# The last block's seven products in another order, tanh in pieces, and unit building with earlier loads

## The chip, the cores and the metric

The kernel runs on one core of one Trainium2 chip. The metric is device time of one launch, in microseconds (us). Engines: TensorE (PE, with its weight loads as PEld), VectorE (DVE), ScalarE (ACT), GpSimd (POOL), and SyncE (SP), whose queue issues nearly all DMAs. Each engine works through its instructions in the order in which they stand.

## The reference

Three stages, all in float32:

```python
# attention with random features, 4 x 8 heads, 576 positions, 64 wide, 128 features
phi(x) = exp(x @ omega.T - |x|^2 / 2 - max) / sqrt(m)
num = phi(q) @ (phi(k).T @ v);  attn = num / (phi(q) @ sum(phi(k)) + 1e-6)
# experts: x is (2304, 512), 8 experts of width 1024
P = exp(x @ w_gate - max), normalized 8 times by rows and columns
out = sum_e P[:, e:e+1] * (relu(x @ w1[e]) @ w2[e])
# last block: 512 -> 2048 -> 512, weights come as float64
h = x @ w_in;  g = h - tanh(h);  return g @ w_out
```

## The kernel before

The 2304 tokens are three thirds of 768 (`stages`, with `s` the third). The attention runs first, then the experts for s = 0, 1, 2, then the last block for s = 0, 1, 2. A float32 product is made of three products of rounded halves: each operand is split into a high half (a cast on ScalarE) and a low half (a difference on GpSimd or VectorE); six matmuls of 384 columns are one `product` (L1255).

Each 2x2 block of products is done with seven products instead of eight (a scheme of the Strassen kind). The seven right operands (`x` units, 0 to 6) are made once per third by `xops`, the seven left ones (`u` units) once per weight block, and are kept in DRAM (`st1` for the experts, `st3` for the last block). Sums of the products give four tiles of 128 x 384, called 11, 12, 21 and 22.

*Unit building.* During the experts' last third (s = 2) the generator `build` (L1166) turns `w_in` from float64 into float32 and makes the `u` units of the last block, in 16 steps (f, c). A step loads two pieces (`rb`, L1176), converts each with `single` (L1115 to 1138: six VectorE instructions, one GpSimd, one ScalarE), makes four sums (L1195 to 1198), and makes seven units of 128 x 128 in tiles `ub`: cast on ScalarE (L1214), difference on GpSimd (L1206), store by `puts` (L1234). `rb` and `ub` share the tag `rs` of pool `rawp`, three slots. Each `yield` is a tick: `between` (L1816) calls `tick` twice after every product of the experts, 14 times for a quad of seven products, and `tick` moves the generators of loads (`weights`), of x units (`xops`; every eighth tick unless `pace[3]`) and of the background (`bg`) by one step. A building step has 19 ticks. So the order of the program is fixed when it is written out; nothing is scheduled on the chip. Meanwhile TensorE works through `quad7` and the experts' second layer (`group`, tile Y, L1436), whose running sums `seven` are copied into the bank first (L1428) and out of it after (L1452) on ScalarE.

*The last block.* For each s there are eight units n (`NF`), 24 in all. `tanh_quad` (L1579) runs seven products into three banks a, b, e. Between two of them `fill` may issue a second-layer group (`l2`, tile l, L1617: 12 matmuls of 512 columns, then an eviction on VectorE, L1644 or L1646). The groups of a pair of units run during the pair after it, three to a unit. Product 0 is copied from a to b on ScalarE (L1586), so that b starts from it. Then come the four tiles, each by `shrink` (L1544): h - tanh(h), with another formula for small |h|, for which a Relu (L1559) gives the mask of `copy_predicated` (L1562). `shrink` issues square, tanh, two more squares, Relu, and the VectorE or GpSimd steps in one go; cast and low half of a tile (`third`) are issued within the next tile's. For the tiles 22 and 21 ("spare"), which lie in SBUF, two steps (L1553, L1554) are on GpSimd, for 11 and 12, which lie in a bank, on VectorE. The `u` units are loaded by `weights` into 16 slots in the order in which they are used, the units of a pair ahead of its four second-layer tiles `v`.

## Time and profile before

| | us |
|---|---|
| median of 3 runs | 2386.59 (2385.42 to 2388.12) |
| the profiled execution | 2392.4, span 2390.6 |
| TensorE busy | 2091.4 (87% of the span) |
| VectorE busy | 1577.1 (66%) |
| GpSimd busy | 1521.3 (64%) |
| ScalarE busy | 1446.7 (61%) |
| mean granted TensorE clock | 0.938 of full speed |

The median of the runs is 5.8 us below the profiled execution. Shares of busy time are means over stages that have different limits; the windows below give them by stretch. The granted clock is in parts of full speed: 1.00 is the upper level, 2.4 GHz, and 0.50 would be the lower, 1.2 GHz, all the time. A line of a wait gives the engine that waits, the tile and line of its instruction, and what released it.

### The profile page before, as it was taken

To read this page: it belongs to the slowest core of one execution; us is meant where nothing else is said; L and a number is where in the kernel's file an instruction comes from. 1 tells how busy PE (TensorE), PEld (TensorE's weight loads), DVE (VectorE), ACT (ScalarE), POOL (GpSimd) and SP (SyncE) were. 2 spreads that over 40 slices of the span, in tenths; PEclk is the share of its full clock that TensorE was granted. 3 is DMA by queue.
4 is the path that set the end of the run, shared out by engine and by line. 5 is a ranking of instruction groups with operands and counts; after the bars stand their busy time and mean duration, and the time that the engine had idled before them with its cause. 6 is when DMAs were issued, how large, how long until landed. Compare 5 with 4: busy or idle time off the path is not lost. (4 is left out here: it accounts for less than half of the span.)

```text
span 2390.6 us, 37677 instructions
## 1 busy us (share of the span) xinstructions
PE 2091.4 (87%) x11264; PEld 1936.5 (81%) x11264; DVE 1577.1 (66%) x3013; ACT 1446.7 (61%) x3563; POOL 1521.3 (64%) x1959
## 2 busy tenths in 40 slices
PE   9989999999999999999987787778995677776868
PEld 7768888899989999999987777778985566676767
DVE  8885779898756576666766566565445666656555
ACT  7874333444347777777676566566775555555554
POOL 7867778778648888888765565556654444334332
PEclk9999999999999999999999888899997888888888
DMA  6548888888768899988986877776774543723341
GB/s 165 151 133 287 302 280 278 309 280 282 245 198 281 310 331 329 347 309 313 350 269 207 272 254 238 253 227 231 251 280 167 194 145 143 266 111 145 115 169 61
DMA packets 394219, 566.44 MB, mean 237 GB/s; under 512 B 75408, under 2 KB 184352, under 8 KB 394016
## 3 DMA queue, kind: packets, MB, share of 16 engines
q1 hardware_dynamic: 387872, 556.63, 68.1%
q10 hardware_dynamic: 6144, 7.40, 0.9%
q8 instruction: 91, 1.49, 0.3%
q14 instruction: 112, 0.92, 0.1%
HBM read 390.81 MB, written 173.09 MB: 236 GB/s over the span
## 5 line engine op out<-in xcount | busy, mean ns | idle before, releaser
L1436 PE MATMUL Y<-h,y 128*128 128x384 f32 x2394 | 512.6, 348 | 102.0 <-ACT Y L1428 101.4
L1261 PE MATMUL b<-x,u 128*128 128x384 f32 x2160 | 468.8, 354 | 143.2 <-ACT b L1586 134.6
L1261 PEld LDWEIGHTS b<-x,u 128*128 128x128 f32 x2160 | 406.6, 200 | 161.9 <-ACT b L1586 143.2
L1436 PEld LDWEIGHTS Y<-h,y 128*128 128x128 f32 x2394 | 440.1, 197 | 116.3 <-ACT Y L1428 115.5
L1617 PE MATMUL l<-v,h 128*128 128x512 f32 x2016 | 489.9, 395 | 2.6 <-ACT x L102 1.8
L1617 PEld LDWEIGHTS l<-v,h 128*128 128x128 f32 x2016 | 381.1, 190 | 80.4 <-ACT x L102 2.1
L1345 POOL TENSOR_TENSOR h<-t,h 128x384 fp32r<-128x384 f32 x223 | 232.2, 1041 | 194.3 <-ACT h L1342 158.4
L1452 ACT COPY seven<-Y 128x384 f32<-128x384 f32 x534 | 247.4, 481 | 148.2 <-PE Y L1436 143.9
L1261 PE MATMUL a<-x,u 128*128 128x384 f32 x1440 | 315.1, 357 | 22.9 <-DMA u<-st 16.7
L1261 PE MATMUL e<-x,u 128*128 128x384 f32 x1440 | 298.4, 343 | 6.7 <-DVE seven L1450 5.7
L1261 PEld LDWEIGHTS a<-x,u 128*128 128x128 f32 x1440 | 276.7, 204 | 28.4 <-DMA u<-st 19.5
L1261 PEld LDWEIGHTS e<-x,u 128*128 128x128 f32 x1440 | 262.6, 194 | 8.2 <-DVE seven L1450 6.2
L1428 ACT COPY Y<-seven 128x384 f32<-128x384 f32 x558 | 262.4, 487 | 4.2 <-DVE seven L1450 4.2
L1345 POOL TENSOR_TENSOR h<-h,h 128x384 fp32r<-128x384 f32 x192 | 201.8, 1054 | 62.4 <-ACT h L1342 51.8
L1568 POOL TENSOR_TENSOR h<-x,h 128x384 fp32r<-128x384 f32 x48 | 51.5, 1073 | 188.8 <-ACT h L1567 188.8
L105 POOL TENSOR_TENSOR v<-rs,v 128x256 fp32r<-128x256 f32 x160 | 123.0, 799 | 54.3 <-ACT v L102 43.1
L1553 POOL TENSOR_TENSOR th<-x,th 128x384 f32<-128x384 f32 x48 | 48.4, 1009 | 154.6 <-ACT th L1552 152.1
L1560 DVE SCALAR_TENSOR_TENSOR x<-t,x 128x384 f32<-128x384 f32 x48 | 56.5, 1178 | 117.5 <-POOL x L1554 117.5
L1342 ACT CAST h<-t 128x384 fp32r<-128x384 f32 x224 | 115.5, 517 | 29.2 <-DVE t L1338 15.6
L1654 DVE SCALAR_TENSOR_TENSOR acc<-l,pt,acc 128x512 f32<-128x512 f32 x144 | 104.7, 743 | 29.4 <-PE l L1617 27.6
L102 ACT CAST u<-s 128x256 fp32r<-128x256 f32 x128 | 49.4, 409 | 105.8 <-POOL u L105 42.0
L105 POOL TENSOR_TENSOR u<-s,u 128x256 fp32r<-128x256 f32 x128 | 97.4, 778 | 22.5 <-ACT u L102 20.1
(270 smaller groups left out, 3799.0 us busy)
## 6 DMA issues: line engine op xcount, KB each, us to landing
u<-st SPq DMA_DIRECT2D x616, 256.0 KB, 5.2
y<-st SPq DMA_DIRECT2D x336, 256.0 KB, 4.9
st<-u SPq DMA_DIRECT2D x224, 256.0 KB, 4.0
rs<-in_moe_w_dram SPq DMA_DIRECT2D x128, 256.0 KB, 4.9
st<-y SPq DMA_DIRECT2D x128, 256.0 KB, 5.8
st<-v SPq DMA_DIRECT2D x96, 256.0 KB, 5.2
rq<-in_moe_w_dram SPq DMA_DIRECT2D x32, 512.0 KB, 4.9
v<-st SPq DMA_DIRECT2D x32, 512.0 KB, 6.2
```

Source lines behind the costliest of these rows:

```text
L102: nc.scalar.copy(dst[:, 0], src)
L105: eng.tensor_tensor(dst[:, 1, i : i + w], src[:, i : i + w], dst[:, 0, i : i + w].bitcast(F32), ALU.subtract)
L1261: nc.tensor.matmul(ps[:, :TB], u[:, wi, c], x[:, xi, c], start=(start and m == 0), stop=(stop and m == 5), skip_group_check=True,)
L1342: nc.scalar.copy(H[k][:, 0], src)
L1345: eng.tensor_tensor(H[k][:, 1], src, H[k][:, 0].bitcast(F32), ALU.subtract)
L1428: nc.scalar.copy(cell[0], xacc[i][:, d])
L1436: nc.tensor.matmul(ps, uw[i, g][0][:, wi, d * P : (d + 1) * P], Hs[g][i][:, hi], start=(n == 0 and not cell), stop=(n == 3 * len(gs) - 1), ...
L1452: nc.scalar.copy(xacc[i][:, d], ps)
L1560: V.scalar_tensor_tensor(s, gb, B1, s, ALU.add, ALU.mult)
L1568: G.tensor_tensor(lo, s, hi.bitcast(F32), ALU.subtract)
L1617: nc.tensor.matmul(ps, hh[f][0][:, hi, t : t + P], u2[n + f][:, wi], start=(f == 0 and i == 0), stop=(f == len(hh) - 1 and i == 2),)
L1654: V.scalar_tensor_tensor(a, ps, p[:, e : e + 1], a, ALU.mult, ALU.add)
```

## The change

*Last block.* `ORDER` becomes 0, 2, 1, 4, 6, 3, 5. `first_product` issues product 0 and the copy to b; `following` issues it for the next unit between products 3 and 5 of this one. `shrink` becomes a class `Tile` whose steps (`even`, `odd`, `squares`, `mask`, `back`, `out`) are issued in pieces, tile 21 before 22, and the last steps of 22 and 12 in the next unit. Second-layer groups stand after products 2, 4 and the next unit's 0, one each. `useq` gives the loads of `u` units the new order.

*Building.* Three `rb` loads are started at the beginning, after the x units of this third are done, and load 2k + 3 + i follows the conversion of piece i of step k. Units are made three to a tile, in pool `xtp` (tag x, five slots, those of the x units' raw tiles) and stored by three DMAs instead of four; a step still has 19 ticks. The x units for the last block's first third are prepared when building is over (`xgo`), one step a tick (`pace[3]`); `convert` waits 16 ticks instead of 6.

```diff
-    ORDER = (0, 2, 1, 4, 3, 5, 6)
+    ORDER = (0, 2, 1, 4, 6, 3, 5)
+    NL = NF * NSB
+    useq = [
+        [(n, 0)] * (n < 2) + [(n, i) for i in range(1, 6)] + [(n + 1, 0)] * (0 < n < NL - 1) + [(n, 6)]
+        for n in range(NL)
+    ]
...
-                    jobs.append(("i", f, None, 0))
+                    jobs.append(("i", s * NF + f, None, 0))
...
-                while a not in built:
+                while len(built) < NF:
                     yield 1
-                for i in range(7):
+                for n, i in useq[a]:
                     while not free1(n1):
                         yield 1
-                    nc.sync.dma_start(tile1(n1).bitcast(F32), st3[a][:, i])
+                    nc.sync.dma_start(tile1(n1).bitcast(F32), st3[n % NF][:, i])
...
-        for _ in range(6 if fine else 1):
+        for _ in range(16 if fine else 1):
...
-        ld(0)
-        ld(1)
-        for _ in range(4):
+        for k in range(3):
+            ld(k)
+        while xbusy:
+            yield
+        for _ in range(10):
             yield
...
+                ld(2 * k + 3 + i)
...
-            for n in range(4):
-                u = rawp.tile([P, 2, 2, P], F32R, tag="rs", name=f"ub{k}_{n}", bufs=3)
-                xs = [src[i] for i in ORDER[2 * n : 2 * n + 2]]
+            for n in range(3):
+                xs = [src[i] for i in ORDER[3 * n : 3 * n + 3]]
+                u = xtp.tile([P, 3, 2, P], F32R, tag="x", name=f"ub{k}_{n}")
                 for o, x in enumerate(xs):
                     nc.scalar.copy(u[:, o, 0], x)
+                    if o == 1:
+                        yield
                 if put:
                     put()
                 put = finish(n - 1) if n else None
                 late.append((u, xs))
                 yield
-                if n == 2:
-                    put()
-                    put = None
-                    ld(2 * k + 2)
-            final = finish(3)
-            yield
+            final = finish(2)
             put()
             yield
             final()
-            ld(2 * k + 3)
...
+    class Tile:
+        def __init__(self, x, spare, name, key):
+            self.x, self.spare, self.name, self.key, self.h = x, spare, name, key, []
+            self.u, self.ga, self.gb = (tmp(i, f"t{i}_{name}") for i in range(3))
+            self.th = xtp.tile([P, TB], F32, tag="xo", name=f"th{name}", bufs=3)
+
+        def even(self):
+            nc.scalar.activation(self.u, self.x, AF.Square)
+            nc.scalar.activation(self.th, self.x, AF.Tanh)
+
+        def odd(self):
+            x, u, th = self.x, self.u, self.th
+            if self.spare:
+                self.s = x
+                nc.gpsimd.tensor_tensor(th, x, th, ALU.subtract)
+                nc.gpsimd.tensor_tensor(x, u, x, ALU.mult)
+            else:
+                self.s = tmp(3, f"t3_{self.name}")
+                nc.vector.tensor_tensor(self.s, u, x, ALU.mult)
+                nc.vector.tensor_tensor(th, x, th, ALU.subtract)
+
+        def squares(self):
+            nc.scalar.activation(self.gb, self.u, AF.Square, bias=bsq[:, 1:2])
+            nc.scalar.activation(self.ga, self.u, AF.Square, scale=CS, bias=bsq[:, 0:1])
+
+        def mask(self):
+            nc.scalar.activation(self.u, self.u, AF.Relu, bias=bsq[:, 2:3])
+
+        def back(self):
+            V, s = nc.vector, self.s
+            V.scalar_tensor_tensor(s, self.gb, B1, s, ALU.add, ALU.mult)
+            V.scalar_tensor_tensor(s, self.ga, A1, s, ALU.add, ALU.mult)
+            V.copy_predicated(s, self.u.bitcast(U32), self.th)
+
+        def out(self):
+            self.h.append(hslot(f"h{self.name}", self.key))
+            hi, lo = self.h[0][:, 0], self.h[0][:, 1]
+            nc.scalar.copy(hi, self.s)
+            nc.gpsimd.tensor_tensor(lo, self.s, hi.bitcast(F32), ALU.subtract)
+
+    lastq = []
+
+    def first_product(n, last):
+        a, b = qbank(f"a_{n}"), qbank(f"b_{n}")
+        product(a, 0, True, False, last)
+        nc.scalar.copy(b[:, :TB], a[:, :TB])
+        return a, b
+
+    def tanh_quad(n, key, last, ab, fill, following):
+        a, b = ab
+        e = qbank(f"e_{n}")
         A, B, EE = (x[:, :TB] for x in (a, b, e))
         V = nc.vector
+        if lxp:
+            x22, x21 = (lxp[0].tile([P, TB], F32, tag="x", name=f"x2{i}_{n}", bufs=3) for i in (2, 1))
+        else:
+            both = xtp.tile([P, 2, TB], F32, tag="x", name=f"x2_{n}")
+            x22, x21 = both[:, 0], both[:, 1]
+        b22, b12 = lastq or (None, None)
+        lastq.clear()
+        product(e, 2, True, False, last)
+        nc.scalar.copy(x22, EE)
+        if b22:
+            b22.out()
         fill(0)
+        product(b, 1, False, False, last)
+        nc.scalar.copy(x21, B)
+        if b12:
+            b12.mask()
+            b12.back()
         fill(1)
+        product(a, 4, False, True, last)
+        t11 = Tile(A, False, f"11_{n}", (*key, 0))
+        t11.even()
+        t11.odd()
+        t11.squares()
+        t11.mask()
+        t11.back()
+        if b12:
+            b12.out()
         fill(2)
+        product(e, 6, False, True, last)
+        t11.out()
+        V.tensor_tensor(x21, EE, x21, ALU.add)
+        t21 = Tile(x21, True, f"21_{n}", (*key, 0))
+        t21.even()
+        t21.odd()
+        t21.squares()
         fill(3)
         product(b, 3, False, False, last)
+        V.tensor_tensor(x22, B, x22, ALU.add)
+        t22 = Tile(x22, True, f"22_{n}", (*key, 1))
+        t22.even()
+        t22.odd()
+        t21.mask()
+        t22.squares()
+        t21.back()
         fill(4)
+        ab = following()
+        fill(5)
         product(b, 5, False, True, last)
+        t12 = Tile(B, False, f"12_{n}", (*key, 1))
+        t12.even()
+        t22.mask()
+        t22.back()
+        t21.out()
+        t12.odd()
+        t12.squares()
+        lastq.extend((t22, t12))
         fill(6)
+        return [[t11.h, t21.h], [t12.h, t22.h]], ab
 
...
-                pace[3] = Q < 2 or Q == NQ - 1
+                pace[3] = Q < 2 or Q == NQ - 1 or s == NSB - 1 and not bg
...
-                if Q == NQ // 4:
+                if Q == NQ // 4 and s < NSB - 1:
+                    xgo[0] += 1
+                if Q > 1 and s == NSB - 1 and not bg and xgo[0] < NSB:
                     xgo[0] += 1
...
+                    elif k in ((3, 5, 6) if turning else (0, 2, 5)):
...
+                def following():
+                    if not s and not n or s == NSB - 1 and n == NF - 1:
+                        return None
+                    over = n == NF - 1
+                    state["x0"] += 7 * over
+                    ab = first_product(f"{s}_{n + 1}", n == NF - 2)
+                    state["x0"] -= 7 * over
+                    return ab
+                if not s and n < 2:
+                    ab = first_product(f"{s}_{n}", False)
+                    if not n:
+                        second(1)
+                blocks, ab = tanh_quad(f"{s}_{n}", (s, n2), n == NF - 1, ab, fill, following)
```

On TensorE, around the turn from unit 5 to unit 6 of the last third, these rows stand before (a, b and e are the banks with their unit's number, l a second-layer group, u and x the units):

```order
L1261 MATMUL b_5_26699<-x_25733,u_26513 128x384 x6
L1261 MATMUL e_5_26698<-x_25799,u_26515 128x384 x6
L1261 MATMUL a_6_26907<-x_25053,u_26829 128x384 x6
L1261 MATMUL e_6_26908<-x_25585,u_26831 128x384 x6
L1261 MATMUL b_6_26909<-x_25609,u_26833 128x384 x6
L1261 MATMUL a_6_26907<-x_25643,u_26835 128x384 x6
L1617 MATMUL l_26959<-v_26541,h_2_4_26690 128x512 x3
```

And now:

```order
L1266 MATMUL e_5_26683<-x_25647,u_26518 128x384 x6
L1266 MATMUL b_5_26637<-x_25692,u_26520 128x384 x6
L1266 MATMUL a_6_26800<-x_25009,u_26522 128x384 x6
L1666 MATMUL l_26809<-v_26171,h_2_2_26376 128x512 x3
L1666 MATMUL l_26809<-v_26184,h_2_2_26326 128x512 x3
L1666 MATMUL l_26809<-v_26210,h_2_3_26576 128x512 x3
L1666 MATMUL l_26809<-v_26459,h_2_3_26509 128x512 x3
L1266 MATMUL b_5_26637<-x_25719,u_26524 128x384 x6
L1266 MATMUL e_6_26863<-x_25523,u_26849 128x384 x6
```

Product 0 of unit 6 (a_6) moved ahead of a second-layer group and the last product of unit 5.

On ScalarE, around the copy b<-a of unit 6, before (L1551 is the square, L1552 tanh, L1555 and L1556 the two squares with a bias, L1559 the Relu, L1567 the cast to the high half; t_21 and the like belong to the tile of that name):

```order
L1567 CAST h_2_5_26860<-x_2_5_26779 128x384
L1559 ACTIVATE t_12_2_5_26849<-t_12_2_5_26849,bsq 128x384
L1551 ACTIVATE t_21_2_5_26888<-x_2_5_26733 128x384
L1552 ACTIVATE th_2_5_26891<-x_2_5_26733 128x384
L1555 ACTIVATE t_21_2_5_26890<-t_21_2_5_26888,bsq 128x384
L1556 ACTIVATE t_21_2_5_26889<-t_21_2_5_26888,bsq 128x384
L1567 CAST h_2_5_26898<-t_12_2_5_26853 128x384
L1559 ACTIVATE t_21_2_5_26888<-t_21_2_5_26888,bsq 128x384
L1586 COPY b_6_26909<-a_6_26907 128x384
L1592 COPY x_2_6_26933<-b_6_26909 128x384
```

And now (L1556 square, L1557 tanh, L1571 and L1572 the two squares, L1575 the Relu, L1586 the cast, L1594 the copy):

```order
L1575 ACTIVATE t_21_2_5_26769<-t_21_2_5_26769,bsq 128x384
L1571 ACTIVATE t_22_2_5_26788<-t_22_2_5_26786,bsq 128x384
L1572 ACTIVATE t_22_2_5_26787<-t_22_2_5_26786,bsq 128x384
L1594 COPY b_6_26801<-a_6_26800 128x384
L1556 ACTIVATE t_12_2_5_26831<-b_5_26637 128x384
L1557 ACTIVATE th_2_5_26834<-b_5_26637 128x384
L1575 ACTIVATE t_22_2_5_26786<-t_22_2_5_26786,bsq 128x384
L1586 CAST h_2_5_26841<-x_2_5_26685 128x384
L1571 ACTIVATE t_12_2_5_26833<-t_12_2_5_26831,bsq 128x384
L1572 ACTIVATE t_12_2_5_26832<-t_12_2_5_26831,bsq 128x384
L1610 COPY x_2_6_26864<-e_6_26863 128x384
```

The copy of b_6 stood behind the Relu of tile 21, the last tile of unit 5; it now stands behind the Relu of tile 21 and two squares of tile 22, ahead of tile 12.

In the load queue, within one building step, before (rb is a load for building, st<-ub a store of units, y and u are loads for the experts):

```order
L1234 DMA st_1_144<-ub_0_17808 128x4x128
L1234 DMA st_1_144<-ub_1_17832 128x4x128
L1176 DMA rb_17864<-in_moe_w_in_dram 128x512
L299 DMA y_17900<-st_10_120 128x512
L277 DMA u_17902<-st_11_89 128x512
L299 DMA y_17900<-st_10_120 128x512
L277 DMA u_17905<-st_11_89 128x512
L1234 DMA st_1_144<-ub_2_17837 128x4x128
L1234 DMA st_1_144<-ub_3_17866 128x2x128
L1176 DMA rb_17909<-in_moe_w_in_dram 128x512
L299 DMA y_17956<-st_10_120 128x512
```

And now:

```order
L1181 DMA rb_18287<-in_moe_w_in_dram 128x512
L304 DMA y_18337<-st_12_122 128x512
L282 DMA u_18339<-st_13_91 128x512
L304 DMA y_18337<-st_11_121 128x512
L282 DMA u_18342<-st_13_91 128x512
L1238 DMA st_2_145<-ub_0_18314 128x6x128
L1238 DMA st_2_145<-ub_1_18344 128x6x128
L1238 DMA st_2_145<-ub_2_18377 128x2x128
L304 DMA y_18461<-st_12_122 128x512
L282 DMA u_18463<-st_14_92 128x512
```

Each rb stood right behind two stores of units; now the loads rb stand ahead of the stores, and the stores are three in a row.

## Rows read from the trace of the kernel before

**Rows 1.** Windows: start:end, length, busy us (count) by engine, clock, DMA, GB/s.

```profile
1230.00:1690.00 460.00, 361.02 (x1817) 348.05 (x1816) 276.94 (x502) 287.65 (x752) 273.57 (x339) 0.89 0.75 242
1700.00:1760.00 60.00, 60.00 (x348) 60.00 (x347) 24.75 (x45) 49.03 (x117) 36.53 (x37) 1.00 0.73 254
1836.00:2354.00 518.00, 379.67 (x1638) 336.58 (x1638) 308.70 (x455) 288.08 (x592) 206.48 (x207) 0.85 0.43 159
2185.00:2354.00 169.00, 128.26 (x546) 113.75 (x546) 95.45 (x146) 90.47 (x189) 58.12 (x58) 0.84 0.33 124
```

**Rows 2.** Waits, 1230 to 1690 us: engine, line, releaser; us, times, longest.

```profile
DVE cb L1122 <- DMA rb<-in_moe_w_in_dram: 103.6, 20, 13.1
...
PE Y L1436 <- ACT Y L1428: 94.6, 31, 9.6
...
ACT ub L1214 <- DMA st<-ub: 84.4, 16, 10.1
```

**Rows 3.** Line L1195: count, ns min/median/max, first and last start.

```profile
L1195 DVE TENSOR_TENSOR sb<-w x16: 275/420/1089, 1241.6 to 1680.6; 128x128 f32<-128x128 f32 x16
```

**Rows 4.** Waits, 1836 to 2354 us.

```profile
PE b L1261 <- ACT b L1586: 128.4, 21, 11.3
```

**Rows 5.** Chain of waits, 2269 to 2285 us: start, us, engine, tile, line.

```profile
2277.12 0.57 DVE t L1561
...
2277.78 0.59 DVE t L1562
...
2278.37 0.45 DVE x L1607
...
2279.86 1.01 POOL th L1553
...
2280.93 1.00 POOL x L1554
...
2282.57 0.39 ACT b L1586
```

**Rows 6.** Timeline of TensorE, 2264 to 2290 us; idle before, releaser.

```profile
2266.48 5.64 PE L1617 MATMUL l<-v,h 128*128 128x512 f32 x24
...
2271.96 1.23 PE L1261 MATMUL b<-x,u 128*128 128x384 f32 x6
...
2274.58 1.32 PE L1261 MATMUL a<-x,u 128*128 128x384 f32 x6 [0.34 <-DMA u<-st]
...
2283.00 2.29 PE L1261 MATMUL b<-x,u 128*128 128x384 f32 x6 [6.05 <-ACT b L1586]
```

**Rows 7.** Timeline of ScalarE: copies b<-a of three units.

```profile
1836.12 0.47 ACT L1586 COPY b<-a 128x384 f32<-128x384 f32 x1
...
2184.79 0.47 ACT L1586 COPY b<-a 128x384 f32<-128x384 f32 x1
...
2354.21 0.47 ACT L1586 COPY b<-a 128x384 f32<-128x384 f32 x1
```

**Rows 8.** DMA issues, 1230 to 1690 us: count, KB, us to landing.

```profile
st<-ub SPq DMA_DIRECT2D x48, 256.0 KB, 4.5
...
rb<-in_moe_w_in_dram SPq DMA_DIRECT2D x30, 256.0 KB, 3.2
...
xt<-xd SPq DMA_DIRECT2D x4, 384.0 KB, 8.0
```

**Rows 9.** Waits of the load queue, 1230 to 1690 us.

```profile
SPq L299 <- PE Y L1436: 98.8, 40, 7.6
```

**Rows 10.** Three lines on VectorE: ns min/median/max, first, last start.

```profile
L1560 DVE SCALAR_TENSOR_TENSOR x<-t,x x48: 548/1333/1361, 1793.5 to 2378.0; 128x384 f32<-128x384 f32 x48
...
L1125 DVE TENSOR_SCALAR cb<-cb x32: 293/296/1092, 1228.2 to 1675.7; 128x256 uint32<-128x256 uint32 x32
...
L1132 DVE SCALAR_TENSOR_TENSOR w<-rb,cb x32: 408/425/1211, 1231.7 to 1677.1; 128x256 f32<-128x256 uint32 x32
```

**Rows 11.** Groups, 1836 to 2354 us: count, busy, mean ns, idle before.

```profile
L1646 DVE TENSOR_TENSOR acc<-l,acc 128x512 f32<-128x512 f32 x44 | 30.0, 682 | 21.0 <-PE l L1617 21.0
```

More of the change, by code (lines that the diff above doesn't have):

```diff
@@ L1255, in product @@
     def product(ps, i, start, stop, last):
+        need(state["n1"], u1, "w")
         need(state["x0"] + i, ux, "x")
@@ L1542, in hslot @@
         return htile(name, kind == "k")
-    def shrink(x, spare, name, key):
-        h = []
-        V, G = nc.vector, nc.gpsimd
-        u, ga, gb = (tmp(i, f"t{i}_{name}") for i in range(3))
-        th = xtp.tile([P, TB], F32, tag="xo", name=f"th{name}", bufs=3)
-        s = x if spare else tmp(3, f"t3_{name}")
-        eng = G if spare else V
-        nc.scalar.activation(u, x, AF.Square)
-        nc.scalar.activation(th, x, AF.Tanh)
-        eng.tensor_tensor(th, x, th, ALU.subtract)
-        eng.tensor_tensor(s, u, x, ALU.mult)
-        nc.scalar.activation(gb, u, AF.Square, bias=bsq[:, 1:2])
-        nc.scalar.activation(ga, u, AF.Square, scale=CS, bias=bsq[:, 0:1])
-        if held:
-            held.pop()()
-        nc.scalar.activation(u, u, AF.Relu, bias=bsq[:, 2:3])
-        V.scalar_tensor_tensor(s, gb, B1, s, ALU.add, ALU.mult)
-        V.scalar_tensor_tensor(s, ga, A1, s, ALU.add, ALU.mult)
-        V.copy_predicated(s, u.bitcast(U32), th)
-        def third():
-            h.append(hslot(f"h{name}", key))
-            hi, lo = h[0][:, 0], h[0][:, 1]
-            nc.scalar.copy(hi, s)
-            G.tensor_tensor(lo, s, hi.bitcast(F32), ALU.subtract)
-        held.append(third)
-        return h
@@ L1585, in tanh_quad @@
-        product(a, 0, True, False, last)
-        nc.scalar.copy(B, A)
-        fill(0)
-        product(e, 2, True, False, last)
-        fill(1)
-        product(b, 1, False, False, last)
-        x21 = spare(0, "x21")
-        nc.scalar.copy(x21, B)
-        fill(2)
-        product(a, 4, False, True, last)
-        h11 = shrink(A, False, f"11_{n}", (*key, 0))
+        if lxp:
[3 more added lines that the diff above has]
+            x22, x21 = both[:, 0], both[:, 1]
@@ L1602, in tanh_quad @@
+        t22 = Tile(x22, True, f"22_{n}", (*key, 1))
[4 more added lines that the diff above has]
+        t21.back()
         fill(4)
+        ab = following()
+        fill(5)
         product(b, 5, False, True, last)
-        h12 = shrink(B, False, f"12_{n}", (*key, 1))
-        fill(5)
-        product(e, 6, False, True, last)
-        V.tensor_tensor(x21, EE, x21, ALU.add)
-        h21 = shrink(x21, True, f"21_{n}", (*key, 0))
+        t12 = Tile(B, False, f"12_{n}", (*key, 1))
@@ L1840, in performer_moe_kernel @@
                 turning = not s and n < 3
-                for i in range(7):
-                    need(state["n1"] + i, u1, "w")
                 def fill(k):
@@ L1846, in fill @@
                     if not s and not n:
-                        second((1, 2, 2, 1, 1, 1, 1)[k])
-                    elif not turning or k > 3:
-                        if k in (1, 3, 4):
-                            second(1)
-                        while k > 4 and len(ready) > (1 if odd else 4):
-                            second(1)
-                    if k == (3 if turning else 1):
-                        ready.extend(coming)
-                        coming.clear()
-                for j, h in enumerate(tanh_quad(f"{s}_{n}", (s, n2), n == NF - 1, fill)):
-                    hh[j].extend(h)
+                        second((2, 2, 1, 1, 1, 1, 1)[k])
+                    elif k in ((3, 5, 6) if turning else (0, 2, 5)):
[11 more added lines that the diff above has]
+                    if not n:
+                        second(1)
+                blocks, ab = tanh_quad(f"{s}_{n}", (s, n2), n == NF - 1, ab, fill, following)
+                for j in range(2):
+                    hh[j].extend(blocks[j])
                 if not s and not n:
@@ L1871, in performer_moe_kernel @@
             state["x0"] += 7
-    held.pop()()
-    second(len(ready))
-    for tt in (3, 4, 5, 0, 1, 2):
-        begun[st, tt] = lbank("l2") if tt > 2 else qbank("l2")
+    b22, b12 = lastq
+    b22.out()
+    b12.mask()
+    b12.back()
+    b12.out()
+    for tt in range(NTS):
+        begun[st, tt] = lbank("l2") if tt < 3 else qbank("l2")
         l2_mm(begun[st, tt], n2 - GF, hh[tt // 3], tt, range(2))
-    ready.extend(coming)
     second(len(ready))
```

23 lines of the change are left out of this document (5 added, 18 removed).

## The prediction

> **What bounds the kernel now.** I read the page's slices first, in which TensorE's digits and its granted clock fall in the second half, and then the windows by stretch, where the reader should look for matmuls per time [rows 1]. From 1700 to 1760 us the third block of the expert layer runs undisturbed: 348 matmuls in 60 us, 0.172 us each, granted clock 1.00. From 1230 to 1690 us the same loop runs with the unit building beside it: 1817 matmuls in 460 us, granted clock 0.89; at 0.172 us they would need 313 us. From 1836 to 2354 us, the last block, 1638 matmuls take 518 us at 0.85. These two stretches are what the change touches, and each has its own bound.
>
> In the building stretch, the waits say who ends the idle time [rows 2]: TensorE waits 94.6 us for ScalarE's copy of the sum into its bank (L1428). That copy is a short instruction behind others: ScalarE itself waits 84.4 us, 16 times, at the casts of the units (L1214) until a store of an earlier tile has landed, once in each building step. VectorE waits 103.6 us, 20 times, at the first conversion (L1122) for its load. One building step lasts (1680.6 - 1241.6) / 15 = 29.3 us [rows 3]; it holds 29.3 x 1817 / 460 = 116 matmuls, 19.9 us at full rate.
>
> In the last block TensorE waits 128.4 us in 21 units, 6.1 us each, for one ScalarE copy, b<-a (L1586) [rows 4]. The chain of waits tells why [rows 5]: the copy needs only product 0 of the new unit, but stands on ScalarE behind the Relu (L1559) of the previous unit's last tile, which waits for two GpSimd steps, which wait for tanh, which waits for the sum x21, which waits for VectorE. After such a wait the next product takes 2.29 us in place of 1.23 [rows 6]: half clock. A unit lasts (2354.21 - 2184.79) / 7 = 24.2 us in the last third and (2184.79 - 1836.12) / 14 = 24.9 us before [rows 7], against a full-rate need of 7 x 1.03 us for the products and 3 x 2.74 us for the second-layer groups (two of them lie between 2266.48 and 2271.96 [rows 6]): 15.4 us.
>
> **The change, part by part.** It adds and removes no arithmetic; per unit the counts of casts, squares, sums and products stay. So every gain is a wait that goes, and every cost a new one.
>
> *Building.* Three loads are started ahead, and load number k+3 is issued as soon as number k is converted. A load is then read two halves later, that is about one step of 19 ticks (1.03 us each at full rate) or 19.9 us after issue; it lands after 3.2 us [rows 8], and even behind the longest wait for a y unit's slot in the load queue, 7.6 us [rows 9], it is there. The unit tiles move from three slots that they shared with those loads to five slots; three tiles a step in five slots means reuse after 1.7 steps, some 33 us, against 4.5 us for a store to land [rows 8]. So both waits go entirely. What is late next is the pair GpSimd and VectorE. A VectorE step whose two inputs lie in SBUF takes 0.55 us alone and 1.33 where it meets GpSimd [rows 10]; the conversions L1125 and L1132 likewise take 0.29 and 0.41 us at the least, 1.09 and 1.21 at the most. So the one waits until the other's instruction ends, and their times add. Per step GpSimd is busy 273.6 / 460 x 29.3 = 17.4 us [rows 1]. VectorE's building steps cost at least 2 x (3 x 0.29 + 3 x 0.41) = 4.2 us, and four 128x128 sums at 0.29 (an estimate from L1125's size) 1.2 us, and the layer's own such step, 19/14 of it in a step at 0.55, 0.8: 6.2 us. Together 23.6 us, more than TensorE's 19.9. I take 25.0, the sum and 6% for turns that are not taken at once; 4.3 us x 16 steps = 68 us less. Bounds: 19.9 us if they overlapped (150 us less), and 29.3 if new waits ate it all (0).
>
> That both directions add is the point where a rule bears on the sum. The Trainium skill, page "SBUF — State Buffer", section "Who interferes with whom", says that the port pair of GpSimd and VectorE is an exclusive lock and that a VectorE instruction with two SBUF inputs contends with GpSimd, one with a single SBUF input (outside the two-port modes) does not. The rows above agree with the first half. By this rule the floor of a step is 23.6 us and the stretch can lose at most 5.7 x 16 = 91 us; without it 150.
>
> *The x units of the last block* are now prepared after the building, one step a tick. Their four loads land after 8.0 us [rows 8] and the first difference stands three ticks (3.1 us) behind the issue on VectorE's in-order queue: 5 us more, once, with everything behind it. Before, eight ticks lay between the steps.
>
> *The last block.* The copy b<-a now follows a product 0 that runs in the middle of the unit before, and stands behind two squares of tile 22. TensorE has b5, product 2, and a second-layer group, 4.8 us, to do before it needs the copy. So the 6.1 us go, and with them the half clock behind them. What is late next is VectorE's queue, which holds all four tiles in order. I follow it round one unit. The two sums: 1.1 us. Then it waits for x21, that is for square, tanh and two GpSimd steps: 2278.37 to 1.00 after 2280.93 is 3.6 us from the first sum's start [rows 5], 2.5 us beyond the sums; behind this wait stand the other tiles and the evictions, and for these TensorE's next groups. Then twelve dependent steps at 0.66 us from start to start (2277.12 to 2277.78 [rows 5]): 7.9. Four PSUM steps at 0.45 (as the sum at 2278.37): 1.8. Three evictions at 0.68 [rows 11]: 2.0. GpSimd has eight steps of 1.0 us in a unit; those that meet VectorE's chain are the two of tile 22 and two of the low halves: 4.0. Sum 19.3; I take 19.5 for the units of the last third. In the first two thirds the x units of the next third and the conversion of the second layer's weights run beside it, hidden in today's waits: GpSimd is busy (206.5 - 58.1) / 14 = 10.6 us a unit there against 58.1 / 7 = 8.3 in the last, VectorE 15.2 against 13.6 [rows 1], together 3.9 us more. Some of it fits into the 2.5 us of waiting; I put 1.5 us on top: 21.0. So 7 x 4.7 + 14 x 3.9 = 33 + 55 = 88 us less. Bounds: 15.4 us by TensorE, plus 0.7 because the first weights after a group now have one product less (1.03 us) of cover than at 2274.58, where they already came 0.34 us late [rows 6], per two units: 16.1; and 12.8 + 8 x 1.0 + 2.5 = 23.3 if all eight GpSimd steps stand in the way. The first two units and the end I leave as they are, with 15 us either way.
>
> Sum, against the profiled execution's 2392.4 us: -68 + 5 - 88 = -151, so 2241. The median is 2386.6, 5.8 us less than the profiled one; I forecast 2386.6 - 151 = 2236 us.
>
> **Rivals.**
> *The pair of GpSimd and VectorE binds harder.* A unit 22.5 us, a step 28 us: 21 x 2.2 + 16 x 1.3 = 67 us less, 2320. For it: today's tile steps L1560 in the SBUF form take 1.33 us at the median [rows 10], so nearly all of them meet GpSimd already. Against: there GpSimd has just been released by the same event, which the new order spreads.
> *TensorE becomes the bound.* A unit 17 us, a step 21 us: 21 x 7.7 + 16 x 8.3 = 294 less, 2093. For it: in stretches between two stalls the building stretch does run at full rate. Against: the sum of 23.6 us above.
> *The loads don't come earlier.* The load queue waits in order, 98.8 us for the slots of the y units (L299) [rows 9]; if new loads and stores stand behind such waits, building stays as it is and only the last block gains: 2386.6 + 5 - 88 = 2304. Against: 7.6 us is the longest of these, under the 19.9 us of lead.
> *Slower: the clock.* Today one long wait per unit costs half clock for one or two products [rows 6]. If the new order breaks this wait into several, and the granted clock of the last block stays near half, TensorE alone needs 2 x 15.4 = 31 us a unit: 23 x 6.4 = 147 more, less 68 and plus 5: 2471. It decides from a granted clock of 15.4 / 27.2 = 0.57 in the last block (there the loss equals the building's gain); today's is 0.85 [rows 1]. Against: products that follow waits of 0.34 us are not slow [rows 6]. The Trainium skill, "TensorE: Matmul & The Clock Gate", section "HAM oscillation — how this bites in real kernels", describes this: a loop whose every turn has a wait pays for the fall of the clock every turn. The trace of before agrees, with 2.29 us after 6.05 us of idling.
>
> **How the numbers follow.** Forecast 0.52, the pair 0.20, TensorE 0.13, loads 0.09, clock 0.06. From the pair I give 0.03 to no change at all. 0.2% (5 us) is about what a measurement of this kernel can tell from nothing. So faster 0.91, same 0.03, slower 0.06. The forecast alone spans 2190 to 2285. For 8 in 10 I leave out the far half of the TensorE case below and the clock above: 2130 to 2325.
>
> **What would show it.** Right: no long wait of the first conversion for rb and none of the unit casts for stores; the building steps 24 to 26 us apart; no long wait of TensorE for b<-a; units 18.5 to 21.5 us apart, VectorE or GpSimd busy for over 80% of them, the SBUF forms of the tile steps near 1 us. Wrong: units at 23 us or at 17, TensorE waiting for weights or x units where the last block begins for more than 20 us, or a granted clock there below 0.8.

## The result and the profile after

The changed kernel takes 2199.84 us (median of 4 runs, 2197.36 to 2202.42); the kernel before, on the same chip, 2387.36 us (2385.42 to 2389.31). The ratio is 0.9215, 95% interval 0.9199 to 0.9231: 187.5 us less. The forecast was 2236 us with a range of 2130 to 2325.

The changed kernel by stretch. The columns are those of [rows 1], the engines in the order PE, PEld, DVE, ACT, POOL; the first line is the building, the second the end of the experts behind it, the third 21 units of the last block.

```profile
1257.00:1593.00 336.00, 310.54 (x1709) 299.26 (x1709) 266.16 (x468) 266.95 (x707) 262.26 (x318) 0.98 0.86 289
1593.00:1685.00 92.00, 75.81 (x409) 73.23 (x408) 43.96 (x71) 63.80 (x153) 48.04 (x51) 0.94 0.83 292
...
1732.00:2159.00 427.00, 355.75 (x1640) 311.74 (x1641) 308.25 (x456) 284.17 (x596) 222.84 (x210) 0.91 0.52 192
```

The same 21 units took 518 us with 1638 matmuls in [rows 1]; now 427 with 1640, and the granted clock rose from 0.85 to 0.91. In the building it rose from 0.89 to 0.98.

The line of a building step's first sum (count, ns min/median/max, first and last start), which was L1195 in [rows 3]; and the waits from 1230 to 1620 us (engine, line, releaser: us, times, longest), which answer to [rows 2].

```profile
L1203 DVE TENSOR_TENSOR sb<-w x16: 276/464/1092, 1257.3 to 1592.8; 128x128 f32<-128x128 f32 x16
```

```profile
POOL h L1350 <- ACT h L1347: 78.1, 60, 5.6
...
PE Y L1441 <- ACT Y L1433: 23.2, 20, 3.3
...
DVE cb L1127 <- DMA rb<-in_moe_w_in_dram: 3.5, 1, 3.5
```

A step now lasts (1592.8 - 1257.3) / 15 = 22.4 us in place of 29.3. The wait of ScalarE's casts for stores (84.4 us) is gone, that of VectorE for its loads is down from 103.6 us to one of 3.5, and TensorE's for ScalarE's copy from 94.6 to 23.2.

Three of the 24 copies b<-a in the timeline of ScalarE (start, us, engine, line), the first, the third and the last, and behind them the first of before; [rows 7] has the third and the last of before.

```profile
1684.76 0.46 ACT L1594 COPY b<-a 128x384 f32<-128x384 f32 x1 [1.27 <-PE a L1266]
...
1732.86 0.47 ACT L1594 COPY b<-a 128x384 f32<-128x384 f32 x1
...
2158.38 0.47 ACT L1594 COPY b<-a 128x384 f32<-128x384 f32 x1
```

```profile
1773.09 0.46 ACT L1586 COPY b<-a 128x384 f32<-128x384 f32 x1 [0.95 <-PE a L1261]
```

A unit lasts (2158.38 - 1732.86) / 21 = 20.3 us on the average, before (2354.21 - 1836.12) / 21 = 24.7. The waits from 1732 to 2159 us:

```profile
DVE x L1579 <- POOL x L1564: 59.1, 22, 3.3
...
PE e L1266 <- DMA u<-st: 48.5, 10, 10.4
...
PE b L1266 <- DVE x L1639: 8.0, 4, 3.7
...
PE l L1666 <- ACT h L1586: 6.3, 4, 1.8
...
PE b L1266 <- ACT b L1594: 2.5, 1, 2.5
```

The wait of [rows 4], 128.4 us in 21 units, is down to one of 2.5 us. TensorE's largest is a new one: product 2 at the start of a pair of units waits for its unit u, ten times. The chain of waits ahead of the longest of these (start, us, what) shows whom the load had waited for:

```profile
1899.47 1.17 DVE x L1580
...
1901.21 0.69 DVE acc L1695
...
1901.92 0.33 SPq L1708
...
1902.35 0.38 SPq L334
...
1902.78 4.43 DMA u<-st
...
1907.26 2.29 PE e L1266 x6
```

L1708 is a store of finished rows, which waits for VectorE's sum; L334 is the fourth v load of a pair, which waits for its ring slot; the u loads of the next pair stand behind both in SP's queue. In this chain the store's wait ended last; L1708 stands there only at the ends of thirds. The queue's own waits from 1732 to 2159 us (line, releaser: us, times, longest) name what holds it elsewhere:

```profile
SPq L334 <- PE l L1666: 78.5, 5, 26.6
...
SPq L155 <- ACT v L107: 42.5, 6, 21.7
```

The v load waits for a second-layer group to free its slot. In the first third the v tiles are still made on the core; there L155, the load of a v tile's source, stands in its place. And product 2, once its weights are there, takes 2.29 us in place of 1.23: the granted clock from 1907.3 to 1909.5 us is 0.50, the lower level.

### The profile page after: what moved, and what is told of

Read it like the earlier page. It is cut to its first block, busy times and chain, and to the rows that moved or that the text cites. A ratio compares the mean times of both kernels' runs of the same rounds, so it can differ in the third digit from the quotient of the medians.

```text
span 2197.3 us, 37735 instructions
## 1 busy us (share of the span) xinstructions
PE 2035.7 (93%) x11264; PEld 1880.2 (86%) x11264; DVE 1588.4 (72%) x3013; ACT 1437.0 (65%) x3563; POOL 1537.9 (70%) x1959
## 4 chain that ended last, share of the span: by engine, by line
PE 58%; DVE 12%; POOL 12%; DMA 7%; issue 5%; ACT 4%; SPq 1%; DVEq 0%; POOLq 0%; ACTq 0%
PE l L1666 15%; PE Y L1441 13%; PE b L1266 11%; PE e L1266 8%; PE a L1266 7%; DMA u<-st 2%; PE X L1441 2%; POOL h L1350 2%; POOL tmp L596 2%; POOL eq L756 1%; DVE x L1579 1%; DMA y<-st 1%; DVE x L1580 1%; DMA xd<-seven 1%; POOL h L1587 1%
## 5 line engine op out<-in xcount | busy, mean ns | idle before, releaser
L1441 PE MATMUL Y<-h,y 128*128 128x384 f32 x2394 | 497.0, 340 | 43.7 <-ACT Y L1433 38.2
L1666 PE MATMUL l<-v,h 128*128 128x512 f32 x2016 | 500.2, 399 | 14.6 <-ACT h L1586 6.3
L1441 PEld LDWEIGHTS Y<-h,y 128*128 128x128 f32 x2394 | 423.6, 190 | 59.0 <-ACT Y L1433 50.2
L1266 PE MATMUL b<-x,u 128*128 128x384 f32 x2160 | 442.5, 340 | 19.6 <-DVE x L1639 9.0
L1266 PEld LDWEIGHTS b<-x,u 128*128 128x128 f32 x2160 | 385.8, 190 | 32.4 <-DVE x L1639 11.8
L1266 PE MATMUL e<-x,u 128*128 128x384 f32 x1440 | 299.9, 344 | 58.4 <-DMA u<-st 48.5
L1350 POOL TENSOR_TENSOR h<-t,h 128x384 fp32r<-128x384 f32 x223 | 232.7, 1044 | 145.1 <-ACT h L1347 120.4
L1266 PE MATMUL a<-x,u 128*128 128x384 f32 x1440 | 293.0, 338 | 3.2 <-DMA u<-st 1.7
L1266 PEld LDWEIGHTS a<-x,u 128*128 128x128 f32 x1440 | 256.3, 190 | 5.5 <-POOL u L110 1.6
L1587 POOL TENSOR_TENSOR h<-t,h 128x384 fp32r<-128x384 f32 x48 | 51.6, 1074 | 112.0 <-ACT h L1586 106.9
L1587 POOL TENSOR_TENSOR h<-x,h 128x384 fp32r<-128x384 f32 x48 | 55.2, 1149 | 97.0 <-ACT h L1586 94.6
L110 POOL TENSOR_TENSOR u<-s,u 128x256 fp32r<-128x256 f32 x128 | 98.2, 783 | 22.6 <-ACT u L107 22.3
L1347 ACT CAST h<-h 128x384 fp32r<-128x384 f32 x192 | 99.0, 516 | 7.5 <-POOL h L1398 5.8
```

Of the source, the lines that this page charges most:

```text
L110: eng.tensor_tensor(dst[:, 1, i : i + w], src[:, i : i + w], dst[:, 0, i : i + w].bitcast(F32), ALU.subtract)
L1266: nc.tensor.matmul(ps[:, :TB], u[:, wi, c], x[:, xi, c], start=(start and m == 0), stop=(stop and m == 5), skip_group_check=True,)
L1347: nc.scalar.copy(H[k][:, 0], src)
L1350: eng.tensor_tensor(H[k][:, 1], src, H[k][:, 0].bitcast(F32), ALU.subtract)
L1441: nc.tensor.matmul(ps, uw[i, g][0][:, wi, d * P : (d + 1) * P], Hs[g][i][:, hi], start=(n == 0 and not cell), stop=(n == 3 * len(gs) - 1), ...
L1587: nc.gpsimd.tensor_tensor(lo, self.s, hi.bitcast(F32), ALU.subtract)
```

## The experiments

**Each part alone.** The first kernel has the new building and the old last block (old order of products, tiles and groups); the second has the new last block and the old building. The lines below are from their edits against the kernel before: the change of `ORDER` is in the second alone, and the line of `useq`, which keeps the old order of the loads, is the first's.

```diff
-    ORDER = (0, 2, 1, 4, 6, 3, 5)
+    ORDER = (0, 2, 1, 4, 3, 5, 6)
...
+    useq = [[(n, i) for i in range(7)] for n in range(NL)]
```

> The new building of the units with the old last block. Theory A (the two edits stand in different stretches and add up): the first b<-a copy of the last block comes 88 us earlier than before (1773 to about 1685), the part behind it keeps its 617 us, the time is about 2387 - 88 = 2299 us, steps of building 22.4 us apart as in the kernel with both edits, granted clock of the building stretch .97 against .89. Rival B (part of the gain of the building is really the last block's, since its loads and x units share the same queue): the part behind the first copy takes under 600 us too, and the time is under 2280.

> The new order of the seven products and of the tanh steps with the old building of the units. Theory A (additive): the building keeps 29.3 us per step, the last block's part behind the first b<-a copy falls from 617 to about 512 us, the time is about 2387 - 105 = 2282 us. Rival B (the new order needs the units that the new building has ready earlier, or the x units that it prepares after building): the last block gains under 80 us, the time is over 2307.

New building alone: 2306.5 us, ratio 0.9665 (0.9651 to 0.968). New last block alone: 2283.0 us, ratio 0.9574 (0.9558 to 0.959). The two losses, 0.0335 and 0.0426, add up to 0.9239 against 0.9215 measured with both, whose interval reaches to 0.9231; theory A holds but for a few us. These kernels were timed on several chips, each beside the kernel before, so small differences are given by the ratios too. First, third and last copy b<-a with the new building alone, and then with the new last block alone:

```profile
1683.14 0.46 ACT L1587 COPY b<-a 128x384 f32<-128x384 f32 x1 [0.55 <-PE a L1262]
...
1745.37 0.47 ACT L1587 COPY b<-a 128x384 f32<-128x384 f32 x1
...
2263.48 0.47 ACT L1587 COPY b<-a 128x384 f32<-128x384 f32 x1
```

```profile
1766.08 0.46 ACT L1595 COPY b<-a 128x384 f32<-128x384 f32 x1 [1.03 <-PE a L1267]
...
1814.43 0.47 ACT L1595 COPY b<-a 128x384 f32<-128x384 f32 x1
...
2242.45 0.47 ACT L1595 COPY b<-a 128x384 f32<-128x384 f32 x1
```

Before, the first copy came at 1773.09 and the third 63.0 us later. With the new building the first comes 90 us earlier, the units keep their 24.7 us; with the new order the first two units take 48.4 us in place of 63.0 and the others 20.4.

**The wait for u.** The next kernel has both parts and lists the loads of a pair's first unit ahead of the fourth v load of the pair before; the one after it also holds the output stores back.

```diff
                 for f in range(g * GF, (g + 1) * GF):
+                    if f == (g + 1) * GF - 1 and p + 1 < NSB * NGM:
+                        jobs.append(("i", 2 * p + 2, None, 0))
...
-            nc.sync.dma_start(out[r : r + P, :], a)
+            stores.append([6, out[r : r + P, :], a])
```

> Both edits, and the loads of a pair's first unit stand in SP's queue before the fourth second-layer (v) load instead of behind it. Theory A (the ten waits of TensorE for u units, 48.5 us, come from SP's queue, where the v load waits for its slot): these waits fall under 10 us in all, the median unit stays 17.5 to 18 us, the time is 2200 - 35 to 45 = 2155 to 2165 us. Rival B (VectorE's queue is the floor at 19.5 us a unit, as the prediction had it): the waits turn into waits of b for x on VectorE, the mean of the 21 units stays above 19.5 and the time is above 2185. Rival C (the transfers themselves are late, or the v loads now come late): waits of l for v of over 20 us appear, time 2180 or more.

> As the kernel before it in this list, and the twelve output stores of the first two thirds are held back by six ticks (about a unit) in SP's queue, so that they don't stand there waiting for VectorE's sums. Theory A (the waits of 9 to 10 us at the thirds' boundaries, 1907 and 2068, are longer than the others since the queue also waits for the stores' sums): another 0 to 10 us, 2150 to 2160. Rival B (with the loads ahead of the blocked v load nothing waits behind the stores): within 3 us of the kernel before it.

2192.1 us, ratio 0.9188 (0.9174 to 0.9202), and 2187.1, ratio 0.9168 (0.9155 to 0.9182). That is 8 and 13 us below the changed kernel (6 and 11 by the ratios; the first interval just meets that of the changed kernel), where theory A expected 35 to 45 for the first; the second step's 5 us lie within the intervals. The waits of TensorE for u were taken away, but others came in their place, those of the second-layer groups. From 1650 to 2180 us of the first of the two:

```profile
PE l L1670 <- ACT h L1590: 27.8, 8, 4.6
...
PE b L1270 <- DVE x L1643: 11.8, 7, 4.2
...
PE l L1670 <- DMA v<-st: 11.4, 2, 6.0
```

None of the three theories names the first of these: at the place where the u load was late, the first group of a pair would have waited for its tile h anyway. h is the tile that the unit before finishes last (L1590 is the cast to its high half). So the next two kernels move the groups one place back, first in the even units, then in all.

```diff
-                    elif k in ((3, 5, 6) if turning else (0, 2, 5)):
+                    elif k in ((3, 5, 6) if turning else (0, 2, 5) if odd else (1, 3, 5)):
...
+                    elif k in ((3, 5, 6) if turning else (1, 3, 5)):
```

> The kernel with the loads ahead and the output stores held back (2187 us), and in the even units of the last block the three second-layer groups stand after the products 1, 4... of the order (places 1, 3, 5) instead of places 0, 2, 5. Theory A (with the loads there in time, the first group of a pair waits for the tile h that the unit before finishes last, 31 us in ten waits of l for ACT's copy of h): these waits fall under 10 us and the time to 2160 to 2172 us. Rival B (VectorE's queue is what is late, and the wait only moves to b or e): the sum of TensorE's waits on VectorE and ACT stays, time 2180 to 2190. Rival C (the later group frees the v slot later and the wait for v comes back): waits of l for v over 15 us.

> The same with places 1, 3, 5 in the odd units too. Theory A: the odd units' groups had no wait, so nothing more is gained, within 5 us of the kernel with the even units alone. Rival B: the groups beside VectorE's longest stretch help there as well, 5 to 15 us faster. Rival C: two products side by side at the start of each odd unit make b wait for the reading of its bank, 5 to 15 us slower.

2161.9 us, ratio 0.906 (0.9047 to 0.9072), and 2156.3, ratio 0.9041 (0.9028 to 0.9053). Theory A held for the first. The second is 6 us faster, between A and B of its expectation, but the intervals overlap. Two windows of the last block of the faster one:

```profile
1850.00:2030.00 180.00, 165.27 (x777) 143.16 (x778) 149.01 (x217) 129.78 (x277) 100.10 (x92) 0.97 0.59 217
2030.00:2120.00 90.00, 85.00 (x412) 73.53 (x411) 74.17 (x112) 66.64 (x144) 46.03 (x43) 1.00 0.46 167
```

TensorE is busy for 92 and 94% of them at a granted clock of 0.97 and 1.00. Its third copy b<-a starts at 1727.74 us and its last at 2115.93: 18.5 us a unit. The waits for b<-a come back in part there: 20.2 us in 16, the longest 2.9, from 1720 to 2120 us. This is the fastest version but for one that measured the same, told of below.

**What sets the building step.** One kernel computes each of the seven low halves twice on GpSimd; one leaves the tiles in their new pool and puts the loads back to their old places; one computes the four sums on VectorE three times.

```diff
                 for o, x in enumerate(xs):
                     G.tensor_tensor(u[:, o, 1], x, u[:, o, 0].bitcast(F32), ALU.subtract)
+                    G.tensor_tensor(u[:, o, 1], x, u[:, o, 0].bitcast(F32), ALU.subtract)
...
-                ld(2 * k + 3 + i)
...
+            ld(2 * k + 2)
             final = finish(2)
...
+            for _ in range(3):
+                V.tensor_tensor(s1, a21, a22, ALU.add)
```

> The changed kernel with each of the seven low halves of a building step computed twice on GpSimd (same result), 7 x 0.50 = 3.5 us more of GpSimd's time per step. Theory A (TensorE sets the step of 22.4 us, busy 310 of 336 us there; GpSimd and VectorE have room): steps of 22.4 to 23.0 us, time 2200 to 2210. Rival B (the times of GpSimd and VectorE add up at their port and set the step, as the prediction had it): steps of 25 to 26 us, time 2240 to 2260.

> The changed kernel with the ub tiles in their new pool, but the loads of the source tiles at their old places (two ahead, issued at the end of a step). Theory A (both waits of before came from the three slots that loads and ub tiles shared; with the loads alone in them the old places are early enough): no wait of VectorE for a load over 3 us, steps of 22.4 to 23 us, time 2200 to 2210. Rival B (a load takes longer to land than the old place leaves it, so the loads ahead are what helps): waits of cb for rb of 3 to 5 us come back in most steps, steps of 25 to 27 us, time 2235 to 2270.

> The changed kernel with the four sums of a building step on VectorE (both inputs in SBUF, 0.28 us each at the least) computed three times over, 2.24 us more of VectorE's time per step. Theory A (GpSimd's time and that of VectorE's steps with SBUF inputs alone add up and set the step of 22.4 us; the kernel with twice the low halves on GpSimd grew by 3.45 us a step for 3.2 to 3.5 added): steps of 24.4 to 25.2 us, time 2230 to 2245. Rival B (GpSimd's own queue sets the step and VectorE has room beside it): steps under 23 us, time under 2212. Rival C (each added step costs the mean that the records show, 0.4 to 0.6 us, so the chain of handing over is what grows): steps of 26 to 27.5 us, time over 2255.

2260.1 us (ratio 0.947, 0.9457 to 0.9483), 2257.1 (0.9457, 0.9444 to 0.947) and 2245.2 (0.9416, 0.9396 to 0.9437). The first sum's line in each of the three, which gives steps of 25.85, 26.06 and 25.1 us (in the third it counts all 48 sums, and its last start is of a third repeat, 1.9 us after the first):

```profile
L1203 DVE TENSOR_TENSOR sb<-w x16: 279/457/1097, 1255.8 to 1643.5; 128x128 f32<-128x128 f32 x16
```

```profile
L1202 DVE TENSOR_TENSOR sb<-w x16: 276/464/1103, 1258.1 to 1649.0; 128x128 f32<-128x128 f32 x16
```

```profile
L1204 DVE TENSOR_TENSOR sb<-w x48: 276/285/1112, 1258.7 to 1636.9; 128x128 f32<-128x128 f32 x48
```

The low halves: rival B, 3.5 us longer for 3.5 us more of GpSimd (3.1 by its shortest records). The sums: theory A but at its upper edge, 2.7 us longer for 2.24 us more of VectorE. Either engine's added time lengthens the step, though neither is busy throughout. Two things can do this: something that the two share, or a chain of steps that wait for one another across both queues. These two kernels don't tell them apart. I had put theory A first for the low halves because TensorE is busy for 310 of 336 us; that was wrong. The loads: rival B. The waits for them were back (waits from 1257 to 1650 us of that kernel):

```profile
DVE cb L1127 <- DMA rb<-in_moe_w_in_dram: 100.0, 15, 14.3
```

So of the 6.9 us a step, taken in this order, 3.2 come from the tiles' own pool (with stores in threes), and 3.7 from the loads ahead.

**Less work for the pair.** On top of the kernel at 2156 us: the low halves and the conversion's two additions on VectorE; the same with one pause less in each of the two full unit groups of a step; the additions alone.

```diff
-        nc.gpsimd.tensor_tensor(xf, xf, h.bitcast(F32), ALU.add)
+        (nc.gpsimd if fine or not r2p else V).tensor_tensor(xf, xf, h.bitcast(F32), ALU.add)
...
-                    G.tensor_tensor(u[:, o, 1], x, u[:, o, 0].bitcast(F32), ALU.subtract)
+                    V.tensor_tensor(u[:, o, 1], x, u[:, o, 0].bitcast(F32), ALU.subtract)
...
-                    if o == 1:
-                        yield
```

> The kernel with the groups at places 1, 3, 5 (2156 us), and in the building the seven low halves and the two additions of the conversion on VectorE instead of GpSimd (0.28 against 0.45 us, 0.41 against 0.72 us at the least): 1.8 us less per step by the sum of both engines. Theory A (the sum sets the step): steps of 20.6 to 21.4 us, where TensorE's own work of about 20.7 us becomes the bound, time 2130 to 2140. Rival B (GpSimd's queue alone): the same steps, but then VectorE's added 2.8 us don't matter either, so the two are told apart by the kernel with the sums three times over, not here. Rival C (VectorE's queue gets too long for the experts' own steps, and TensorE waits for t on VectorE): steps as before, time 2150 to 2170.

> The same with one pause less in each of the two full unit groups of a step (two of the ticks that pace the building), so that the building ends some 25 to 35 us earlier and the x units of the last block are prepared over more of the experts' end. Theory A (TensorE's idle time between the end of building and the last block, about 15 us in 92 and 15 in 47, comes from the x units being bunched there): 10 to 25 us faster than the kernel before it in this list. Rival B (the work of GpSimd and VectorE over the whole stage is the same and only moves): within 8 us of it.

> The kernel with the groups at places 1, 3, 5 (2156 us), and in the building only the two additions of the conversion on VectorE (2 x 0.72 us less on GpSimd, 2 x 0.41 more on VectorE, 0.6 us less in the sum), the seven low halves on GpSimd as before. It asks why moving both gained nothing. Theory A (there VectorE's own queue, busy in 94% of the stretch, became the bound; with 2 us less on it the sum binds again): steps of 21.5 to 21.9 us, time 2144 to 2151. Rival B (the steps of 22.3 us are by now set by TensorE and its hand-overs to ScalarE, whatever GpSimd and VectorE do): steps of 22.2 to 22.7 us, time 2153 to 2163.

2159.3 us (ratio 0.9058, 0.9044 to 0.9071), 2163.7 (0.9073, 0.906 to 0.9085) and 2155.5 (0.9023, 0.901 to 0.9035): no gain that can be told from nothing. With both moved, steps stay at (1596.3 - 1258.1) / 15 = 22.5 us, so theory A fails there; with the additions alone they are (1589.4 - 1259.2) / 15 = 22.0, between A and B, and the time is the same. The window of the building with both moved:

```profile
1257.00:1593.00 336.00, 306.62 (x1702) 295.00 (x1701) 316.57 (x597) 265.00 (x703) 193.73 (x183) 0.99 0.87 289
```

GpSimd is down from 262 to 194 us, but VectorE is up from 266 to 317 of 336, its waits for GpSimd included. That VectorE's queue is the bound then is the likely reading, but no run shows it. With the additions alone the step is 0.3 us shorter than in the kernel before it (22.3), as the sum of both engines in the table below would have it, and some 4 us in 15 steps are too little to be seen in the time. The pauses: rival B.

## Why the forecast came out 36 us too high

The forecast's parts against the two profiled executions, of which the spans differ by 2390.6 - 2197.3 = 193.3 us:

| part | forecast | measured |
|---|---|---|
| up to the first copy b<-a | -68 + 5 = -63 | 1684.8 - 1773.1 = -88.3 |
| first two units | 0, 15 either way | 48.1 - 63.0 = -14.9 |
| 21 units | -88 | (20.26 - 24.67) x 21 = -92.6 |
| end | 0 | 38.9 - 36.4 = +2.5 |

**The building: right mechanism, a term mis-sized.** Both waits went, as forecast, and the kernel with the loads at their old places shows that the loads ahead were needed for it. What binds next is the pair GpSimd and VectorE, as forecast: the kernels with added work show it from both sides. But I took 25.0 us, a sum of 23.6 and 6% for turns that are not taken at once, and the step took 22.4. There was no room for the 6%, and the sum was a little high: I had put GpSimd in with the time for which it is recorded busy, 17.4 us, and with its shortest records it is 16.7. I added up the timelines from 1270 to 1580 us again with each kind of instruction at its shortest, and of VectorE's only those kinds that are longer at some places than at others (most have two inputs in SBUF; three of the conversion's, L1127, L1130 and L1135, have one):

| kernel | GpSimd + VectorE, us per step | step took |
|---|---|---|
| changed | 16.7 + 6.0 = 22.8 | 22.4 |
| low halves twice | 19.8 + 6.1 = 25.9 | 25.85 |
| sums three times | 16.9 + 8.2 = 25.1 | 25.1 |
| loads late | 16.6 + 6.2 = 22.8 | 26.06 |
| both moved to VectorE | 12.3 + 8.7 = 20.9 | 22.5 |
| additions on VectorE | 15.2 + 6.9 = 22.1 | 22.0 |

In the first three rows and the last the sum is the step to 2%. That either engine's added time lengthens the step agrees with the Trainium skill, "SBUF — State Buffer", section "Who interferes with whom", that the pair's port is an exclusive lock. The loss of 103.5 us in 15 steps is beyond the 91 us in 16 that I had called the most by this rule: 23.6 us was no floor. The newer sum isn't one either, since the step took 0.4 us less than it. In 310 us of the changed kernel GpSimd or one of these kinds of VectorE is recorded at work for 275, and neither for 35, while their shortest records add up to 313; so at least 38 us of these lie side by side. The sum is a measure found after the fact, which fits four kernels that share most of their work; that the port alone sets the step, and no chain of hand-overs, is not shown.

**The x units, +5 us: too little.** The building starts 15.7 us later (1257.3 against 1241.6), since it now waits until the x units of its own stage are done and ten ticks more; from its last step to the first copy it takes 92.0 us, before 92.5. So -6.9 x 15 = -103.5, +15.7 and -0.5 make the -88.3. But the later start is no loss by itself: TensorE works meanwhile, 7228 matmuls up to the start against 7123, and the end has the less to do, 409 matmuls against 506. At 0.172 us each [rows 1] these need 70 us of the 92.0, before 87 of the 92.5. So the end lost 5.5 us before and loses 21.6 now, 16 more where I had put 5, and TensorE idles for 16 of its 92 us. Its longest wait there is for a ScalarE copy that stands behind the cast of a tile of the x units, which waits for its load (timelines of ScalarE and TensorE):

```profile
1644.35 0.83 ACT L107 CAST x<-xm 128x768 fp32r<-128x768 f32 x1 [9.48 <-DMA xm<-xd]
...
1645.62 2.29 PE L1441 MATMUL Y<-h,y 128*128 128x384 f32 x6 [8.61 <-ACT Y L1433]
```

I had priced a load on VectorE's queue, and the longest stop came from one on ScalarE's. No run leaves the x units out, so how much of the 16 us is theirs is not shown.

**The last block: the size right, its reason half right.** The wait for b<-a went, with the half clock behind it (TensorE has two groups and not one to do before it needs the copy, 7.5 us and not 4.8), and units of 20.3 us lie between the 19.5 and 21.0 of the forecast. That they do is in part luck. But what is late next is not VectorE's queue round one unit. The kernel with all groups moved runs units of 18.5 us with the same steps on VectorE, so the 19.5 was no floor. Late next are two waits at one place, those of the first product and of the first group of a pair: u behind the v load, or in the first third its source's, in SP's queue (48.5 us, 2.3 a unit), and h of the unit before. Taking away the first alone brought 8 us, both (and the held stores) 38 to 44 (6, and 37 to 42, by the ratios). I had seen that a product less stands ahead of the first weights, and priced this by their 0.34 us of lateness [rows 6] at 0.7 us for two units; 4.6 were measured. What I did not follow is the order in the load queue: these loads stand behind one that in the last two thirds is released only by a group of the pair before, and in the first by the making of a v tile. The signs that I gave came half: the two waits of the building gone, but its steps 22.4 us apart and not 24 to 26; units of 20.3 us and no wait for b<-a, but no engine of the pair busy over 80% (VectorE 308 of 427 us, 72%), and over 20 us of waiting for weights, though spread over the pairs.

**The first two units** gained 14.9 us, at the edge of what I allowed; the new last block alone shows the same with the old building (48.4 us), so it is the new order.

**The rivals.** The pair binding harder (2320) and loads not coming earlier (2304) fell by the steps of 22.4 us. TensorE as the bound (2093) is nearer than I had thought: with loads and groups moved the kernel is at 2156 and TensorE busy for 92 to 94% of the last block. The clock's rival fell: 0.91 there, above the 0.57 from which it would decide.

## What to carry to other kernels

When a wait is taken out, follow each queue that the next instruction depends on, the load queue too: a load that waits for a slot holds back all behind it, and a product that loses one product of cover can wait for ten of them. Where GpSimd and VectorE work side by side in SBUF, take each kind's shortest record, add up all of GpSimd's and those of VectorE's that vary in length, and compare this sum with TensorE's need: here it came out as the step to 2%, with no margin on top, where nothing else bound. When work is moved to another place, count the matmuls of each stretch too: a stretch that takes the same time with less work in it has lost. When a wait is gone and the time hardly moves, look what ended the next wait at the same place, and move both.

## What the runs showed of the hardware

Two lines of VectorE in the changed kernel (count: ns min/median/max). The first has an input in PSUM, the second, in the building, all of them in SBUF:

```profile
L1366 DVE TENSOR_TENSOR t<-e,t x64: 557/557/559, 690.7 to 1676.8; 128x384 f32<-128x384 f32 x64
```

```profile
L1143 DVE SCALAR_TENSOR_TENSOR w<-cb,w x31: 409/1217/1230, 1256.0 to 1590.8; 128x256 f32<-128x256 f32 x31
```

I had expected some spread in both. The one with an operand in PSUM never varies by over 2 ns in 64, whatever GpSimd does; the other takes 0.41 us alone and in most cases three times as long: it then mostly starts as one GpSimd step ends and lies beside the next. At 1322.09 us, for one, that next step ends 0.94 us after its start, and its own record 0.28 us later. So the recorded busy time of both engines together, 528 us in a stretch of 336, says little of their need.
